# Attention inside two fused feed-forward layers: the two heads of a pair at partitions 0 and 64, scores as row tiles, outputs and kv as column tiles of the array

## The chip, the cores and the metric

One core of a Trainium2 chip runs one program. The metric is the device time of one execution in microseconds (us); shorter is better. The engines are called as in the profile: PE is TensorE's matmul side and PEld its weight loads, DVE is VectorE, ACT is ScalarE, POOL is GpSimd, and SP issues most DMAs.

## What is computed

The reference, cut to what matters (4 batches, 8 heads, 768 tokens, head size 48; all inputs are given in 32-bit floats except the four weight matrices, which are 64-bit floats):

```python
for t in range(S):
    state = alpha[:, :, t, :, None] * state + einsum('bhd,bhe->bhde', k[:, :, t], v[:, :, t])
    y[:, :, t] = einsum('bhd,bhde->bhe', q[:, :, t], state)
x = y.transpose(0, 2, 1, 3).reshape(3072, 384)
h = x @ w_in                 # 384 -> 2048
g = where(h >= 1, h, where(h <= -1, 0, (h + 1) ** 2 / 4))
x = g @ w_out                # 2048 -> 384
h = x @ w2_in; out = maximum(0.01 * h, h) @ w2_out
```

## The kernel before

**The two layers.** The 3,072 tokens are cut into 24 chunks of 128, three chunks to a tile of 384 columns, so eight tiles a layer. For each tile `gemm_in` (L451, matmuls on L460) makes 16 slices of the hidden layer, each with nine matmuls of 384 columns (three pieces of the contraction, three passes of a high and a low part of the operands), and `gemm_out` (L482, matmuls on L500 in the first layer and L502 in the second) adds each slice to the output with nine more. The non-linear function and the split into high and low part (L471 to L478) run on ACT, DVE and POOL. The 64-bit weights become 32-bit ones on ACT, DVE and POOL (`tick`, L207; the helpers at L27 to L40): the first layer's while the first tile is worked on, the second layer's later.

**The attention.** A chunk c belongs to batch c % 4. It is worked as seven or eight stages, for the eight heads as four pairs; R = 96 is the size of a pair, two heads of 48 side by side on the partitions. `st_alpha` (L274) transposes alpha on PE into a PSUM bank (tile `Tal`, L263), and DVE makes from it the running products in two sets of scans, `kt` (L278) and `qt` (L290), with the chunk's total `tot` and its bookkeeping in `good` (L286) between them; POOL scales the running state by `tot` (L293). The scans `qt` are the last to read the bank of `Tal`. `st_k` and `st_q` transpose k and q (`Tk`, `Tq`) and multiply. `st_qab` (L306) makes on ACT two copies of q, each with the other head of the pair set to zero (through the 0/1 mask `bdm`), so that a matmul over all 96 partitions gives the scores of one head. `st_scores` (L325) does this in two halves of two pairs: a matmul of 256 columns takes both heads, and DVE multiplies by the causal mask into `S` (L336). `st_ktok` transposes the keys back, `st_kv` (L342) multiplies keys and values of a pair (96 by 96, of which `bdm` keeps two blocks on DVE, L362) and POOL adds the result to the state (L363). `st_y` (L366) makes the outputs from the state (L374) and from `S` and `vpad` (L376), which holds each head's v with 48 columns of zeros beside it; ACT and DVE write them as high and low part into `xt`, the input of the first layer, and three small DMAs per chunk carry the fourth pair to the partitions from 96 up.

**What sets the order.** PE's order is the program's (a manual schedule for PE; the other engines' orders are made by a scheduler). The first three chunks stand in the list PRE ahead of the layers. From then on the stages of STEADY are dealt out over 27 half-steps to three chunks, one group of nine layer matmuls to a half-step: `slot = i * SLOTS // cnt`, in which cnt is the number of stage words. After the first stretch the attention's PSUM tiles come from a pool of three banks in turn, one bank to a tile (two halves of the scores are two tiles); a new tile waits until the last reader of the tile three before it is done:

```python
"al.0 q.0 qab.0 al.1 t k.0 sc0.0 k.1 sc1.0 t q.1 qab.1 t kt.0 "
...
STEADY = "al.1 sc0.0 k.1 sc1.0 qq.1 kt.0 y.0 kv.0"
```

## Time and profile before

| what | value |
|---|---|
| median of 3 runs (lowest, highest) | 1026.54 us (1025.8, 1028.24) |
| the profiled execution: its time, its span | 1027.63 us, 1026.0 us |
| PE, busy share of the span | 985.7 us, 96% |
| PEld | 965.3 us, 94% |
| DVE | 483.3 us, 47% |
| ACT | 492.0 us, 48% |
| POOL | 397.6 us, 39% |
| mean granted TensorE clock | 0.987 of full speed |
| chain of waits: PE, DVE, DMA | 86%, 6%, 3% of the span |

The span runs from the first to the last instruction of the profiled execution. A matmul of 32-bit floats outside the layers runs as two passes, each with its own weight load, so a group of two matmuls stands as x4 in the trace. Matmuls are pipelined, and a record covers more time than the array is taken up: what a group costs is read from the distance between starts, not from its own length. The first matmul after a group of another kind is recorded some 0.03 us after that group's last pass started, and its own successor shows the true pace.

### The profile page before, as it was taken

Reading aid. Unit: us, or ns where it says so; the run is one execution under the profiler, and the core shown is the slowest. Engines: PE = TensorE matmul, PEld = TensorE weight load, DVE = VectorE, ACT = ScalarE, POOL = GpSimd, SP = SyncE. Lnnn points to the kernel's source line nnn. Section 1 sums busy time; section 2 is a strip of 40 time slices with the busy share of each in tenths; the row PEclk is TensorE's granted clock in tenths of the full one; section 3 lists DMA queues with packets and bytes.
Section 4 is the critical chain, followed back from the end, with each engine's and each line's share of the span. In section 5 each row is a group of like instructions: output and inputs, shape, how many; then the busy total and the mean of one; then the engine's idle time right before and its main releaser. Section 6 shows DMA issues by size and latency. Waiting matters only on the chain.

```text
span 1026.0 us, 15727 instructions
## 1 busy us (share of the span) xinstructions
PE 985.7 (96%) x5874; PEld 965.3 (94%) x5874; DVE 483.3 (47%) x965; ACT 492.0 (48%) x966; POOL 397.6 (39%) x402
## 2 busy tenths in 40 slices
PE   6688799999999999999999999999999999999997
PEld 5587699999999999999999998999999999999997
DVE  7999955456475556555553445232322212121211
ACT  4476654554555465555555773333333333333332
POOL 2477843344434343433333333333333333333332
PEclk9799899999999999999999999999999999999999
DMA  9865542133344253342322435120201000000000
GB/s 190 197 147 138 135 111 47 35 100 88 91 110 104 72 137 87 99 105 76 98 61 62 130 101 167 32 70 24 70 30 40 15 10 23 1 24 1 24 1 27
DMA packets 133651, 78.95 MB, mean 77 GB/s; under 512 B 104384, under 2 KB 122304, under 8 KB 133568
## 3 DMA queue, kind: packets, MB, share of 16 engines
q1 hardware_dynamic: 121472, 52.71, 21.4%
q10 hardware_dynamic: 12096, 25.17, 7.9%
q8 instruction: 48, 0.79, 0.3%
q14 instruction: 35, 0.29, 0.1%
HBM read 59.77 MB, written 15.73 MB: 74 GB/s over the span
## 4 chain that ended last, share of the span: by engine, by line
PE 86%; DVE 6%; DMA 3%; issue 2%; POOL 1%; ACT 1%; SPq 1%; POOLq 0%; ACTq 0%; DVEq 0%
PE h L460 37%; PE acc L502 19%; PE acc L500 18%; PE sc L329 3%; PE y L376 3%; PE y L374 2%; DVE z L40 1%; DMA raw<-in_moe_w_in 1%; PE kv L350 1%; DMA ends<-in_alpha 1%; POOL z L35 1%; DVE z L31 1%; PE Tal L263 1%; PE Tq L263 1%; DVE good L528 1%
## 5 line engine op out<-in xcount | busy, mean ns | idle before, releaser
L460 PE MATMUL h<-xt,wi 128*128 128x384 f32 x2304 | 458.7, 343 | 8.3 <-DVE wi L183 3.2
L478 POOL TENSOR_TENSOR gg<-t,gg 128x384 fp32r<-128x384 f32 x256 | 268.6, 1050 | 490.8 <-ACT gg L477 484.7
L460 PEld LDWEIGHTS h<-xt,wi 128*128 128x128 f32 x2304 | 405.2, 189 | 12.8 <-DVE wi L183 3.8
L500 PE MATMUL acc<-gg,wo 128*128 128x384 f32 x1152 | 234.1, 347 | 0.2 <-POOL gg L478 0.2
L502 PE MATMUL acc<-wo,gg 128*128 128x384 f32 x1152 | 223.5, 338 | 0.0
L477 ACT ACTIVATE gg<-t 128x384 fp32r<-128x384 f32 x256 | 134.2, 525 | 183.3 <-DVE t L473 105.3
L502 PEld LDWEIGHTS acc<-wo,gg 128*128 128x128 f32 x1152 | 205.2, 188 | 0.0
L500 PEld LDWEIGHTS acc<-gg,wo 128*128 128x128 f32 x1152 | 202.5, 189 | 1.9 <-POOL gg L478 0.5
L476 DVE TENSOR_TENSOR t<-h,t 128x384 f32<-128x384 f32 x128 | 71.1, 557 | 272.9 <-ACT t L475 272.9
L475 ACT ACTIVATE t<-h 128x384 f32<-128x384 f32 x128 | 62.9, 492 | 180.4 <-PE h L460 180.4
L473 DVE SCALAR_TENSOR_TENSOR t<-t,h 128x384 f32<-128x384 f32 x128 | 70.2, 548 | 118.4 <-ACT t L472 113.5
L471 ACT ACTIVATE t<-h,half 128x384 f32<-128x384 f32 x128 | 73.8, 577 | 76.2 <-PE h L460 61.2
L35 POOL TENSOR_TENSOR z<-z,raw 128x384 int32<-128x384 int32 (+1 forms) x56 | 68.6, 1224 | 62.2 <-DVE z L32 39.0
L472 ACT ACTIVATE t<-t 128x384 f32<-128x384 f32 x128 | 67.1, 524 | 4.0 <-ACT t L471 1.0
L329 PE MATMUL sc<-qab,kt 96*128 96x256 f32 x192 | 54.7, 410 | 12.8 <-DVE S L336 5.7
L376 PE MATMUL y<-S,vpad 128*96 128x128 f32 x384 | 55.9, 272 | 2.1 <-DVE S L336 2.1
L329 PEld LDWEIGHTS sc<-qab,kt 96*128 96x128 f32 x192 | 38.2, 206 | 17.7 <-DVE S L336 6.3
L376 PEld LDWEIGHTS y<-S,vpad 128*96 128x96 f32 x384 | 46.4, 162 | 2.8 <-DVE S L336 2.8
L40 DVE SCALAR_TENSOR_TENSOR z<-raw,z 128x384 int32<-128x384 int32 (+1 forms) x56 | 44.6, 796 | 3.9 <-POOL z L35 1.6
L29 ACT ACTIVATE raw<-raw 128x384 int32<-128x384 uint32 (+1 forms) x56 | 33.7, 602 | 17.3 <-DMA raw<-in_moe_w_in 12.9
L31 DVE TENSOR_SCALAR z<-z 128x384 f32<-128x384 f32 (+1 forms) x56 | 30.5, 544 | 22.8 <-ACT z L30 22.6
L278 DVE TENSOR_TENSOR_SCAN kt<-Tal,zcol 96x127 f32<-96x127 f32 x96 | 32.4, 396 | 14.1 <-PE Tal L263 14.1
(69 smaller groups left out, 669.4 us busy)
## 6 DMA issues: line engine op xcount, KB each, us to landing
raw<-in_moe_w_out SPq DMA_DIRECT2D x16, 384.0 KB, 3.2
raw<-in_moe_w_in ACTq DMA_DIRECT2D x12, 512.0 KB, 4.2
raw<-in_moe_w_out ACTq DMA_DIRECT2D x16, 384.0 KB, 3.3
nat<-in_alpha SPq DMA_DIRECT2D x24, 192.0 KB, 3.2
nat<-in_k SPq DMA_DIRECT2D x24, 192.0 KB, 4.3
nat<-in_q SPq DMA_DIRECT2D x24, 192.0 KB, 4.5
vpad<-in_v SPq DMA_DIRECT2D x48, 96.0 KB, 2.6
raw<-in_moe_w_in SPq DMA_DIRECT2D x12, 384.0 KB, 4.5
```

The lines of the kernel that those rows point to most:

```text
L35: add_eng.tensor_tensor(out=z, in0=z, in1=low, op=ALU.add)
L329: nc.tensor.matmul(ps[:, i].rearrange("p e t -> p (e t)"), cs[c]["kt"][:, a, :], cs[c]["qab"][:, a].rearrange("p e t -> p (e t)"),)
L376: nc.tensor.matmul(y[:, a, :], vp[:, 2 * a + e, :], d["S"][:, a, e, :], start=first and e == 0, stop=e == 1)
L460: nc.tensor.matmul(h, w[:, wl, kk, f0:f0 + 128], xt[:, kk, xl, :], start=cnt == 0, stop=cnt == 3 * KD - 1,)
L471: nc.scalar.activation(out=t, in_=h, func=ACTF.Relu, bias=half, scale=0.5)
L472: nc.scalar.activation(out=t, in_=t, func=ACTF.Square)
L473: gi = nc.vector.scalar_tensor_tensor(out=g, in0=t, scalar=1.0, in1=h, op0=ALU.min, op1=ALU.max)
L476: gi = nc.vector.tensor_tensor(out=g, in0=h, in1=t, op=ALU.max)
L477: hi = nc.scalar.activation(out=gg[:, HI], in_=g, func=ACTF.Copy)
L478: lo = nc.gpsimd.tensor_tensor(out=gg[:, LO], in0=g, in1=gg[:, HI].bitcast(F32), op=ALU.subtract)
L500: nc.tensor.matmul(acc[d][:, :N], w[:, wl, mi, d * 128:(d + 1) * 128], gg[:, xl], start=st, stop=sto)
L502: nc.tensor.matmul(acc[d][:, :DM], gg[:, xl, d * C:(d + 1) * C], w[:, wl, mi, :], start=st, stop=sto)
```

## The change

The heads of a pair lie at partitions 0 and 64 (HP = 64; R is now 112, with 16 unused partitions between, X = 16). Scores: one matmul per head over 48 partitions, 128 columns, the two heads of a pair in different halves of the array's rows (a tile of 64 by 128) and into two banks, all eight in one stage; the copies `qab`, their mask and the stage `qab` are gone. Outputs from `S`: one matmul per head with 64 or 48 output rows in different halves of the array's columns (a tile of 128 by 64), after the four matmuls with the state. kv: likewise, per head 48 columns, and DVE adds into the two blocks of the state itself (ACT copies them for the first four chunks). POOL scales the state in two halves. alpha, k and q land in three fixed tiles with 64 places to a head, whose gaps POOL sets once; v is one DMA per chunk instead of two; the pieces of the first weight matrix come in four DMAs instead of two, and six small DMAs per chunk instead of three move the fourth pair. The pools of the attention are closed when it is done, and the pool `natp` is opened in their place.

```diff
-    R = 2 * D
+    HP = 64
+    R = HP + D
+    X = HP - D
...
+    states = [stp.tile([R, NP, R], F32, name=f"state{i}") for i in range(B)]
+    vs = [stp.tile([128, H, HP], F32, name=f"v{i}") for i in range(2)]
+    nats = [stp.tile([128, 3, H, HP], F32, name=f"nat{i}") for i in range(3)]
+    heads = [slice(HP * e, HP * e + D) for e in range(2)]
...
-            r3 = KD * R + 32 * i
-            (cq if layer else nc.sync).dma_start(out=t[:R], in_=wsrc[layer, kind][i * R:(i + 1) * R, cols])
-            (cq if layer else nc.sync).dma_start(out=t[R:], in_=wsrc[layer, kind][r3:r3 + 32, cols])
+            for e in range(2):
+                r0, r1 = (2 * i + e) * D, (2 * KD + e) * D + X * i
+                nc.sync.dma_start(out=t[HP * e:HP * e + D], in_=wsrc[layer, kind][r0:r0 + D, cols])
+                nc.sync.dma_start(out=t[HP * e + D:HP * e + HP], in_=wsrc[layer, kind][r1:r1 + X, cols])
...
-            nc.gpsimd.tensor_tensor(out=st, in0=st, in1=tot.to_broadcast([R, NP, R]), op=ALU.mult)
+            for h in heads:
+                nc.gpsimd.tensor_tensor(
+                    out=st[h, :, h], in0=st[h, :, h], in1=tot[h].to_broadcast([D, NP, D]), op=ALU.mult
+                )
...
-        for e in range(2):
-            nc.scalar.activation(out=qab[:, :, e, :], in_=qt, func=ACTF.Copy, scale=bdm[:, e * D:e * D + 1])
...
-    def st_scores(c, hf):
-        ps = bank("sc").rearrange("p (a e t) -> p a e t", a=2, e=2)
...
+    def st_scores(c):
+        kt, qt = cs[c]["kt"], cs[c]["qt"]
+        ps = [bank(f"sc{e}") for e in range(2)]
+        for a in range(NP):
+            for e, h in enumerate(heads):
+                nc.tensor.matmul(ps[e][:, a * C:(a + 1) * C], kt[h, a, :], qt[h, a, :])
+        S = sp.tile([128, 2, NP, C], F32, tag="S", name="S")
+        for e in range(2):
+            nc.vector.tensor_tensor(
+                out=S[:, e],
...
-            nc.tensor.matmul(
-                ps[:R, a * R:(a + 1) * R],
...
+            for e in range(2):
+                n = D if e else HP
+                nc.tensor.matmul(
+                    kv[HP * e:HP * e + n, a, :],
+                    cs[c]["kn"][:, a, HP * e:HP * e + n],
+                    vs[c % 2][:, 2 * a + e, :D],
+                )
         st = states[c % B]
-        if c < B:
-            nc.vector.tensor_tensor(out=st, in0=kv, in1=bd, op=ALU.mult)
-        else:
-            kvd = sp.tile([R, NP, R], F32, tag="kvd", name="kvd", bufs=1)
-            nc.vector.tensor_tensor(out=kvd, in0=kv, in1=bd, op=ALU.mult)
-            nc.gpsimd.tensor_tensor(out=st, in0=st, in1=kvd, op=ALU.add)
+        for h in heads:
+            if c < B:
+                nc.scalar.activation(out=st[h, :, h], in_=kv[h], func=ACTF.Copy)
+            else:
+                nc.vector.tensor_tensor(out=st[h, :, h], in0=kv[h], in1=st[h, :, h], op=ALU.add)
...
-        for a in (3, 0, 1, 2):
-            if not first:
-                nc.tensor.matmul(y[:, a, :], states[c % B][:, a, :], d["qt"][:, a, :], start=True, stop=False)
+        if not first:
+            for a in range(NP):
+                nc.tensor.matmul(
+                    y[:, a, :], states[c % B][:, a, :], d["qt"][:, a, :],
...
+        for a in range(NP):
             for e in range(2):
+                n = D if e else HP
                 nc.tensor.matmul(
-                    y[:, a, :], vp[:, 2 * a + e, :], d["S"][:, a, e, :], start=first and e == 0, stop=e == 1
+                    y[HP * e:HP * e + n, a, :], vs[c % 2][:, 2 * a + e, :n], d["S"][:, e, a, :],
...
-    STEADY = "al.1 sc0.0 k.1 sc1.0 qq.1 kt.0 y.0 kv.0"
+    STEADY = "al.1 sc.0 k.1 q.1 kt.0 y.0 kv.0"
```

With seven words instead of eight a chunk still takes nine half-steps, and the words move within them. On PE, between the transposes of k and of q of one chunk (`h` and `acc` are the groups of the layers; `Tal` of the same chunk stands two such groups and one scores stage ahead of `Tk` in both), before:

```order
L500 MATMUL acc_1571<-gg,wo_1162 128x384
L263 MATMUL Tk<-ident,nat 96x128 x4
L460 MATMUL h<-xt,wi_258 128x384 x9
L329 MATMUL sc<-qab,kt 128x256 x2
L500 MATMUL acc_1569<-gg,wo_1162 128x384 x3
L500 MATMUL acc_1570<-gg,wo_1162 128x384 x3
L500 MATMUL acc_1571<-gg,wo_1162 128x384 x3
L263 MATMUL Tq<-ident,nat 96x128 x4
L460 MATMUL h<-xt,wi_258 128x384 x9
L318 MATMUL ktok<-ident,kt 128x96 x4
```

and in the changed kernel:

```order
L494 MATMUL acc_1637<-gg,wo_1221 128x384
L267 MATMUL Tk<-ident,nat_128 112x128 x4
L454 MATMUL h<-xt,wi_267 128x384 x9
L267 MATMUL Tq<-ident,nat_128 112x128 x4
L494 MATMUL acc_1635<-gg,wo_1221 128x384 x3
L494 MATMUL acc_1636<-gg,wo_1221 128x384 x3
L494 MATMUL acc_1637<-gg,wo_1221 128x384 x3
L454 MATMUL h<-xt,wi_267 128x384 x9
L318 MATMUL ktok<-ident,kt 128x112 x4
```

The second half of the scores has left this place: `Tq` comes one layer group and a half of the scores earlier, and both halves of the scores stand together in the stage between `Tal` and `Tk`. Since each half takes a bank, `Tk` is now the third tile after `Tal` and gets its bank, where before the second half of the scores got it.

The outputs on PE, with the state (L374, now L369) and with `S` (L376), before:

```order
L374 MATMUL y<-qt,state_123 96x128
L376 MATMUL y<-S,vpad_127 96x128 x2
L374 MATMUL y<-qt,state_123 96x128
L376 MATMUL y<-S,vpad_127 96x128 x2
L374 MATMUL y<-qt,state_123 96x128
L376 MATMUL y<-S,vpad_127 96x128 x2
L374 MATMUL y<-qt,state_123 96x128
L376 MATMUL y<-S,vpad_127 96x128 x2
L460 MATMUL h<-xt,wi_258 128x384 x9
L350 MATMUL kv<-vpad_127,kn 96x96 x4
```

and in the changed kernel:

```order
L369 MATMUL y<-qt,state_122 112x128 x4
L376 MATMUL y<-S,v_126 64x128
L376 MATMUL y<-S,v_126 48x128
L376 MATMUL y<-S,v_126 64x128
L376 MATMUL y<-S,v_126 48x128
L376 MATMUL y<-S,v_126 64x128
L376 MATMUL y<-S,v_126 48x128
L376 MATMUL y<-S,v_126 64x128
L376 MATMUL y<-S,v_126 48x128
L454 MATMUL h<-xt,wi_267 128x384 x9
L349 MATMUL kv<-v_126,kn 64x48
L349 MATMUL kv<-v_126,kn 48x48
```

The number of matmuls of the outputs is the same (four with the state, eight with `S`), the first four of them now come first, and the eight go in turn to the two halves of the columns; kv has eight matmuls of 48 columns for four of 96.

On POOL, where the state is scaled (`gg` is the low part of a layer's hidden slice, `z` a piece of weights), with the semaphores that each row waits for, before:

```order
L363 TENSOR_TENSOR state_125<-state_125,kvd 96x384 [waits DVE_49]
L478 TENSOR_TENSOR gg<-t,gg 128x384 [waits Activation_49]
L293 TENSOR_TENSOR state_123<-state_123,tot 96x384 [waits DVE_49]
L478 TENSOR_TENSOR gg<-t,gg 128x384 [waits PE_49,Activation_49] x2
L276 MEMSET kt 96x4 [waits PE_49]
```

and in the changed kernel:

```order
L472 TENSOR_TENSOR gg<-t,gg 128x384 [waits PE_49,Activation_49]
L298 TENSOR_TENSOR state_123<-state_123,tot 48x4x48 [waits DVE_49]
L298 TENSOR_TENSOR state_123<-state_123,tot 48x4x48 [waits Pool_49]
L472 TENSOR_TENSOR gg<-t,gg 128x384 [waits PE_49,Activation_49,Pool_49]
L472 TENSOR_TENSOR gg<-t,gg 128x384 [waits PE_49,Activation_49]
```

The one scaling of 384 elements has become two of 192, the second waits for the first's own semaphore, and the addition of kv (L363) is gone from POOL.

## Rows read from the trace of the kernel before

**Rows 1.** Stretches: us, then busy us of PE, PEld, DVE, ACT, POOL; PEclk, DMA share, GB/s

```profile
0.00:137.00 137.00, 105.72 (x589) 93.88 (x590) 121.16 (x244) 81.94 (x165) 84.98 (x86) 0.91 0.72 163
137.00:512.00 375.00, 375.00 (x2404) 368.24 (x2403) 210.09 (x470) 203.15 (x396) 143.59 (x156) 1.00 0.35 88
```

**Rows 2.** Timeline of PE over one chunk: start us, length us, engine, line, operation

```profile
207.64 0.60 PE L263 MATMUL Tal<-ident,nat 128*96 128x128 f32 x4
...
209.67 1.03 PE L329 MATMUL sc<-qab,kt 96*128 96x256 f32 x4
...
212.12 0.60 PE L263 MATMUL Tk<-ident,nat 128*96 128x128 f32 x4
...
216.60 0.60 PE L263 MATMUL Tq<-ident,nat 128*96 128x128 f32 x4
...
218.62 0.49 PE L318 MATMUL ktok<-ident,kt 96*128 96x96 f32 x4
...
220.57 0.38 PE L374 MATMUL y<-qt,state 96*96 96x128 f32 x2
220.79 0.60 PE L376 MATMUL y<-S,vpad 128*96 128x128 f32 x4
...
224.79 0.84 PE L350 MATMUL kv<-vpad,kn 128*96 128x96 f32 x8
...
227.07 1.75 PE L460 MATMUL h<-xt,wi 128*128 128x384 f32 x9
228.66 0.27 PE L263 MATMUL Tal<-ident,nat 128*96 128x128 f32 x1
```

**Rows 3.** Timeline around L536, whose matmul has one output row (128*1)

```profile
964.68 0.34 PE L502 MATMUL acc<-wo,gg 128*128 128x384 f32 x1
964.94 0.09 PEld L536 LDWEIGHTS good<-good,ones_r 128*1 128x1 f32 x2 [0.25 <-issue]
964.95 0.20 PE L536 MATMUL good<-good,ones_r 128*1 128x20 f32 x2
965.36 0.52 PE L460 MATMUL h<-xt,wi 128*128 128x384 f32 x2
```

**Rows 4.** Weight loads from 137 us on, by line: ns min/median/max

```profile
L329 PEld LDWEIGHTS sc<-qab,kt x136: 186/188/193, 138.6 to 517.2; 96*128 96x128 f32 x136
L376 PEld LDWEIGHTS y<-S,vpad x256: 161/162/164, 149.8 to 505.3; 128*96 128x96 f32 x128
```

**Rows 5.** Timelines of PE and DVE after a `Tal`, an undisturbed chunk

```profile
249.67 0.60 PE L263 MATMUL Tal<-ident,nat 128*96 128x128 f32 x4
252.18 0.79 DVE L286 SCALAR_TENSOR_TENSOR good<-tot,good 96x4 f32<-96x4 f32 x1
252.90 1.59 DVE L290 TENSOR_TENSOR_SCAN qt<-Tal,rtot,zcol 96x128 f32<-96x128 f32 x4
```

**Rows 6.** Timelines of PE, DVE and POOL after a `Tal`, a disturbed chunk

```profile
157.72 0.60 PE L263 MATMUL Tal<-ident,nat 128*96 128x128 f32 x4
160.56 1.77 DVE L286 SCALAR_TENSOR_TENSOR good<-tot,good 96x4 f32<-96x4 f32 x1
162.25 1.59 DVE L290 TENSOR_TENSOR_SCAN qt<-Tal,rtot,zcol 96x128 f32<-96x128 f32 x4
160.51 0.83 POOL L293 TENSOR_TENSOR state<-state,tot 96x384 f32<-96x384 f32 x1 [2.95 <-DVE tot L284]
161.29 1.01 POOL L478 TENSOR_TENSOR gg<-t,gg 128x384 fp32r<-128x384 f32 x1
```

**Rows 7.** L286 from 137 us on: count, ns min/median/max

```profile
L286 DVE SCALAR_TENSOR_TENSOR good<-tot,good x17: 500/792/1967, 139.6 to 513.9; 96x4 f32<-96x4 f32 x17
```

**Rows 8.** Groups of instructions, by form, first 137 us: busy us, mean ns

```profile
L359 DVE TENSOR_TENSOR state<-kv,bdm 96x384 f32<-96x384 f32 x4 | 2.2, 542 | 0.0
L310 ACT ACTIVATE qab<-qt,bdm 96x512 f32<-96x512 f32 x14 | 9.3, 713 | 10.0 <-DVE qt L304 10.0
```

**Rows 9.** Chain of waits, opening: start us, us, what

```profile
8.86 0.42 SPq L159
```

More of the change, by code (lines that the diff above doesn't have):

```diff
@@ L101, in fast_path, with to_second @@
     pt = ctx.enter_context(tc.tile_pool(name="pt", bufs=3, space=bass.MemoryType.PSUM))
+    first = ctx.enter_context(ExitStack())
+    rawp = first.enter_context(tc.tile_pool(name="rawp", bufs=3))
+    tp = first.enter_context(tc.tile_pool(name="tp", bufs=2))
+    sp = first.enter_context(tc.tile_pool(name="sp", bufs=2))
+    stp = first.enter_context(tc.tile_pool(name="stp", bufs=1))
+    second = {}
+    def to_second():
+        first.close()
+        second["natp"] = ctx.enter_context(tc.tile_pool(name="natp", bufs=3, reuse_waits="tile"))
     x2d = dram.tile([128, KD, NT], F32, name="x2d")
@@ L113, in fast_path @@
     warm = const.tile([128, 1], F32, name="warm")
-    states = [const.tile([R, NP, R], F32, name=f"state{i}") for i in range(B)]
-    vpad = [const.tile([128, H, R], F32, name=f"vpad{i}") for i in range(2)]
-    nat = {}
+    states = [stp.tile([R, NP, R], F32, name=f"state{i}") for i in range(B)]
+    vs = [stp.tile([128, H, HP], F32, name=f"v{i}") for i in range(2)]
+    nats = [stp.tile([128, 3, H, HP], F32, name=f"nat{i}") for i in range(3)]
+    heads = [slice(HP * e, HP * e + D) for e in range(2)]
     fetched = set()
@@ L193, in load_z @@
         else:
-            t = natp.tile([128, DM], F32, tag="nat", name="zo")
+            t = second["natp"].tile([128, DM], F32, tag="nat", name="zo")
         cq.dma_start(out=t, in_=wz[kind, g][i])
@@ L304, in st_q @@
         nc.vector.tensor_tensor(out=qt, in0=ps, in1=qt, op=ALU.mult)
-    def st_qab(c):
-        qt = cs[c]["qt"]
-        qab = tp.tile([R, NP, 2, C], F32, tag="qab", name="qab", bufs=1)
-        for e in range(2):
-            nc.scalar.activation(out=qab[:, :, e, :], in_=qt, func=ACTF.Copy, scale=bdm[:, e * D:e * D + 1])
-        cs[c]["qab"] = qab
     def st_ktok(c):
@@ L388, in st_y @@
             for kk in range(KD):
-                nc.sync.dma_start(
-                    out=xt[R:, kk, :, cols].bitcast(F32), in_=xs[32 * kk:32 * kk + 32, :, :].bitcast(F32)
-                )
+                for e in range(2):
+                    nc.sync.dma_start(
+                        out=xt[HP * e + D:HP * e + HP, kk, :, cols].bitcast(F32),
+                        in_=xs[HP * e + X * kk:HP * e + X * (kk + 1), :, :].bitcast(F32),
+                    )
     tilesA = [(3 * i, 3) for i in range(NCH // 3)]
@@ L521, in alpha_ends @@
         w = B * H * S * D // (128 * NE)
-        t = natp.tile([128, w], F32, tag="nat", name="ends")
+        t = second["natp"].tile([128, w], F32, tag="nat", name="ends")
         nc.sync.dma_start(
@@ L544, in load_x2 @@
         xt = get_xt((1, j), n)
-        x = natp.tile([128, KD, N], F32, tag="nat", name="x2r")
+        x = second["natp"].tile([128, KD, N], F32, tag="nat", name="x2r")
         nc.sync.dma_start(out=x, in_=x2d[:, :, c0 * C:c0 * C + N])
@@ L589, in fast_path @@
         nc.scalar.activation(out=warm, in_=half, func=ACTF.Relu)
-        for t in vpad:
-            tv = t.rearrange("p (a two) (z d) -> p a two z d", two=2, z=2)
-            for e in range(2):
-                nc.vector.memset(tv[:, :, e, 1 - e, :], 0.0)
-        bt = bdm
-        ones.memset(bt, 1.0)
-        ones.affine_select(out=bt[:, :D], in_=bt[:, :D], pattern=[[0, D]], compare_op=ALU.is_ge, fill=0.0, base=D - 1, channel_multiplier=-1)
-        ones.affine_select(out=bt[:, D:], in_=bt[:, D:], pattern=[[0, D]], compare_op=ALU.is_ge, fill=0.0, base=-D, channel_multiplier=1)
+        for t in vs:
+            nc.vector.memset(t[:, :, D:], 0.0)
+        for t in states:
+            nc.vector.memset(t, 0.0)
+        for t in nats:
+            ones.memset(t[:, 0, :, D:], 1.0)
+            ones.memset(t[:, 1:, :, D:], 0.0)
         pos = 0
```

61 lines of the change are left out of this document (17 added, 44 removed), and 3 rows, old and new, of the table PRE.

## The prediction

> **What bounds the kernel now.** I read the table of stretches first, then PE's timeline over one chunk, then the timelines of DVE and POOL at the places where PE will wait for them. From 137 to 512 us PE is busy without a gap [rows 1]: 375.00 of 375.00 us, the clock at its full 2.4 GHz, no other engine over 60%. There a microsecond taken from PE's queue is a microsecond of the run, and one added, or waited, likewise. Before 137 us DVE is the busy engine (121.16 of 137 us, PE 105.72): weights are converted and PE waits, so less PE work buys nothing there. After 512 us there is no attention (its last matmuls start at 505 [rows 4]). The layers' own matmuls are unchanged.
>
> One chunk in the middle stretch shows what the attention takes from PE [rows 2]. A layer group of nine matmuls goes from 227.07 to 228.66, 1.59 us. `Tq` to `ktok` is 2.02 us with one such group, so four transposes take 0.43. `Tal` to `Tk` is 4.48 with two layer groups, so half of the scores takes 0.87, both 1.74. `ktok` to `y` is 1.95: 0.36. `y` to kv is 4.22: 2.63 for 24 passes, 0.11 each, of which the 16 with `S` take 1.75. kv to the next `Tal` is 3.87: 0.69.
>
> **What the change does on PE, per chunk.** The passes do not become fewer or shorter: 16 of 128 columns for the scores (before, 8 of 256), 16 of 128 for the outputs with `S`, 16 of 48 for kv (before, 8 of 96). A gain can come only from the array working on two halves at a time. No row shows that, so I bound it: without overlap a pass of 128 columns costs its 0.11; with full overlap two passes share it. A head has two passes, and PE keeps its order, so the second pass of one head can run beside the first of the next: 16 passes then take 9 steps, not 8. I take the overlapped end, because the pairs share neither rows (scores) nor columns (outputs, kv), and because loads and matmuls of different passes already run side by side: a load of 96 columns lasts 0.162 us by its record [rows 4] and the passes still follow every 0.11.
>
> Against it stands the price of going to a smaller tile and back, which one place shows [rows 3]. The matmul on L536 has one output row. Its weight load starts 0.26 us after the start of the last layer matmul, and from that start to the second layer matmul behind it are 0.68 us. Two ordinary distances are 2 x 0.177 (1.59 / 9), its own two tiny passes some 0.05: 0.28 us is lost, an unhidden load of 128 columns on the way out included. The first load on the way in comes on top: loads of 128 and 96 columns differ by 26 ns [rows 4], 0.8 ns a column, so some 0.10 for 128 columns and 0.05 for 64. Three groups per chunk pay this:
>
> - scores: 0.28 + 0.10 + 9 x 0.11 = 1.37 instead of 1.74: -0.37
> - outputs with `S`: 0.28 + 0.05 + 9 x 0.11 = 1.32 instead of 1.75: -0.43 (the passes with the state are as before)
> - kv: a pass of 48 columns streams for some 0.04, its load takes 0.05: 0.28 + 0.05 + 9 x 0.05 = 0.78 instead of 0.69: +0.09
> - `ktok` has 112 columns for 96: 0.36 x 112 / 96, +0.06. The other transposes stream the same 128 columns.
>
> That is -0.65 for a chunk with kv and -0.80 for the last four, which have neither kv nor `ktok`. From 137 us on there are 14 and 4: -9.1 and -3.2, together -12.3 us.
>
> **The new wait.** `Tk` now needs the bank of `Tal`, which DVE frees with its last `qt` scan. From the start of `Tal` to `Tk` PE will have 4.48 - 0.87 + 1.37 = 4.98 us. In an undisturbed chunk the scans end at 252.90 + 1.59 = 254.49, 4.82 after `Tal` [rows 5]: just in time. In a disturbed one they end at 163.84, 6.12 after it [rows 6], and PE would stand 1.14 us with all its queue behind it. The reason is `good`, an operation on four numbers per partition: it starts 0.05 after POOL's scaling of the state and ends only when that and the `gg` straight behind it are over, 1.77 us; where POOL has the scaling alone it takes 0.79 [rows 5]. So DVE gets through only when POOL pauses. The change cuts the scaling into two, the second waiting for the first's semaphore: that is a pause after about half of 0.83. Its price is not in the trace: between 0 (DVE gets through after 0.42, `good` at some 0.45, the scans some 1.3 us earlier, at 4.8) and the full 1.14 per disturbed chunk. I take the pause, since a wait of POOL for itself must let its first half finish. About eight of the 17 chunks that begin in this stretch are disturbed (the median of `good`, 0.792, is still the undisturbed value, the longest 1.967 [rows 7]), some by weight conversions that DVE takes in between; for those, and for `Tq`, which needs the first scores' bank after `Tk`, I leave 3.5 us.
>
> **Beside PE.** Before 137 us DVE loses four operations (`state<-kv`, 2.2 us [rows 8]), which go to ACT, and ACT loses 9.3 us of `qab` that stood between DVE and the scores. Against that SP issues more: six more DMAs ahead of the first conversions, at 0.42 each [rows 9], 2.5 us if none were hidden. I take -2.5 for the stretch, bounds +2.5 and -7 (DVE's 2.2 and half of `qab`'s 9.3). From 137 us on ACT (54%), POOL (38%) and DVE's two half additions for `kvd` are covered by PE; they matter only through the wait above. The DMAs of v and of the fourth pair fall in the same stretch and have most of a chunk's 21 us to land.
>
> **Sum.** -12.3 + 3.5 - 2.5 = -11.3. The profiled execution took 1027.63 us, 1.1 above the median of 1026.54; its span is 1026.0. 1027.63 - 11.3 - 1.1 gives **1015 us** as a median. A measurement of this kernel tells some 0.2%, 2 us, from no change.
>
> **Rivals.**
>
> *The halves do not run side by side.* The tiles are named, but each pass still takes its turn. Then scores are 0.38 + 16 x 0.11 = 2.14 (+0.40), outputs +0.34, kv 0.33 + 16 x 0.05 = 1.13 (+0.44), `ktok` +0.06: +1.24 in 14 chunks, +0.74 in four, 20.3 us; less 2.5: **1044**, slower. For it: no row shows two matmuls at once, and three entries and exits per chunk are certain. The point that decides is the length of a step of two passes: PE breaks even at (4.18 - 0.39 - 0.33 - 0.78 - 0.06) / 18 = 0.146 us, between 0.11 and 0.22.
>
> *Loads take turns, matmuls overlap.* Two loads of 128 columns need 0.21, so the scores gain nothing (+0.40); 64 and 48 columns need 0.09, less than the 0.11 of a step, so outputs keep -0.43; kv goes at 0.09 a pair, 0.33 + 8 x 0.09 = 1.05 (+0.36). With `ktok` +0.39 in 14 chunks and -0.03 in four, 5.3 us, no wait for `Tk`, less 2.5: **1029**. The Trainium skill (TensorE: Matmul & The Clock Gate, "LDWEIGHTS (loading the stationary operand)") has the time of a load go by its columns and not its rows, as rows 4 have it; the same skill (TensorEngine Tiling (Array Packing), "Key Properties") says that different tiles load and multiply in parallel, which speaks against this rival. No run here shows either for two tiles.
>
> *DVE does not get through in POOL's pause.* Then the disturbed chunks wait for `Tk`: eight times some 1.2 us, 9.6, with the 3.5 for the rest: -12.3 + 13.1 - 2.5 = -1.7, **1025**: PE's gain is eaten by the bank that DVE holds. For it: in rows 6 POOL starts `gg` without a pause and DVE is passed over. Against it: there POOL did not wait for itself. The Trainium skill (TensorEngine Tiling (Array Packing), "PSUM Bottleneck") warns that tiling speeds up TensorE and not the emptying of PSUM; that would be this case.
>
> **How the numbers follow.** The forecast gets 0.40, DVE passed over 0.17, loads in turn 0.19, no overlap 0.15, and 0.09 is left for an opening or a wait that goes otherwise (it may go either way). The forecast's own range is 1008 (no waits left, the opening at its better bound) to 1021. The range over the cases is 1008 to 1042: it holds the first three and leaves out most of the last. Faster by over 0.2%: 0.40 + a third of 0.17 + half of 0.09 and a little from loads in turn, 0.51, which I cut to 0.48 for what I cannot see; same 0.13; slower 0.39.
>
> **What would show it.** Starts of `sc` passes 0.05 us apart on average and a chunk's period of 20.4 us for 21.0 say that the halves overlap; 0.11 apart, with a period over 22 us, that they do not. Weight loads starting 0.26 us after the last layer matmul at each of the three groups confirm the price of a tile; at once, as elsewhere, refute it. `good` at 0.45 us confirms the pause, at 0.9 or 1.8 the third rival, with PE waiting for `qt` ahead of `Tk`. PE's last gap before the dense stretch earlier than 137 us confirms the opening. I am wrong if a step of two passes takes over 0.146 us, or if the dense stretch has waits of over 12 us.

## The result and the profile after

| | before | after |
|---|---|---|
| median | 1026.49 us (4 runs) | 1011.07 us (4 runs, 1010.6 to 1013.11) |
| ratio, 95% interval | | 0.9851 (0.9832 to 0.987) |
| profiled execution: time, span | 1027.63, 1026.0 us | 1010.68, 1008.9 us |

The time fell by 15.4 us, and the forecast of 1015 us lies 4 us beside it. That nearness is partly luck. The table cuts both spans where the same group of `h` begins (one group for each slice of the hidden layer; the 16th stands ahead of the dense stretch, at the 112th no attention is left).

| stretch of the span | before | after | difference | predicted |
|---|---|---|---|---|
| start to group 16 | 137.08 us | 142.79 us | +5.7 | -2.5 |
| group 16 to 112 | 419.66 | 405.40 | -14.3 | -8.8 |
| of it the attention's groups, waits for `Tk` included | 116.07 | 104.02 | -12.05 | -8.8 |
| of it the layers' own matmuls | 303.6 | 301.4 | -2.2 | 0 |
| group 112 to the end | 469.2 | 460.7 | -8.5 | 0 |

The attention gained more than forecast, the opening lost instead of gaining, and 8 to 9 us come from where nobody had looked: the pace of the layers' own matmuls.

From the page of the changed kernel, its span, busy times and the shares of the chain of waits:

```profile
span 1008.9 us, 16606 instructions
...
PE 956.6 (95%) x6226; PEld 923.7 (92%) x6226; DVE 469.3 (47%) x979; ACT 467.3 (46%) x926; POOL 385.8 (38%) x409
...
PE 81%; DVE 7%; DMA 4%; ACT 2%; SPq 2%; issue 2%; POOL 1%; ACTq 0%; DVEq 0%; POOLq 0%
```

PE is busy 29 us less and is off the chain of waits more often than before (81% for 86%). The stretches, with the columns of [rows 1]:

```profile
0.00:143.00 143.00, 100.22 (x687) 90.03 (x688) 116.80 (x244) 77.80 (x159) 84.95 (x90) 0.83 0.66 156
143.00:512.00 369.00, 366.37 (x2688) 346.32 (x2687) 208.17 (x499) 186.18 (x367) 135.34 (x163) 1.00 0.34 89
512.00:700.00 188.00, 187.01 (x1107) 184.99 (x1107) 72.83 (x119) 95.41 (x190) 63.26 (x61) 1.00 0.28 87
700.00:950.00 250.00, 250.00 (x1445) 249.70 (x1444) 61.44 (x100) 89.79 (x176) 85.12 (x81) 1.00 0.08 25
```

The dense stretch, 375.00 of 375.00 us in [rows 1], now has 2.63 us of gaps in 369. In the opening no engine is full: DVE is busy 116.80 of 143 us, where it had 121.16 of 137. The last row becomes important below: 1,445 matmuls in 250 us without any attention.

The timeline of PE over one chunk, to be laid beside [rows 2]:

```profile
300.22 0.60 PE L267 MATMUL Tal<-ident,nat 128*112 128x128 f32 x4
...
302.34 1.16 PE L330 MATMUL sc<-qt,kt 48*128 48x128 f32 x16
303.43 1.84 PE L454 MATMUL h<-xt,wi 128*128 128x384 f32 x9
305.17 0.65 PE L267 MATMUL Tk<-ident,nat 128*112 128x128 f32 x4
...
310.83 0.55 PE L318 MATMUL ktok<-ident,kt 112*128 112x112 f32 x4
...
312.80 1.04 PE L369 MATMUL y<-qt,state 112*112 112x128 f32 x8
313.77 1.09 PE L376 MATMUL y<-S,v 128*64 128x128 f32 x16
...
316.56 0.67 PE L349 MATMUL kv<-v,kn 128*64 128x48 f32 x16
...
320.40 0.60 PE L267 MATMUL Tal<-ident,nat 128*112 128x128 f32 x4
```

The 16 passes of the scores begin at 302.34, and the next layer group at 303.43. Taken singly from the trace, they start in pairs: 302.342 and 302.349, 302.555 and 302.562, then a pair every 0.105 to 0.112 us, eight steps for 16 passes, of which the first is twice as long. The outputs with `S` do the same (313.771 and 313.778, the next pair 0.15 us on, then a pair every 0.109 us). From `Tal` to `Tal` are 20.18 us with nine layer groups in between, 21.0 before. The Trainium skill (TensorEngine Tiling (Array Packing), "Key Properties") says that different tiles load and multiply in parallel; the trace agrees, 7 ns apart.

Each group's cost beyond the layers' matmuls around it (from the start of the last layer matmul ahead to the second behind, less two distances of 0.1733 us), median per chunk:

| group | before | after | difference | predicted |
|---|---|---|---|---|
| scores | 1.738 us | 1.297 us | -0.44 | -0.37 |
| outputs, passes with the state included | 2.645 | 2.096 | -0.55 | -0.43 |
| kv | 0.707 | 0.794 | +0.09 | +0.09 |
| `ktok` | 0.371 | 0.405 | +0.03 | +0.06 |
| `Tal`, `Tq` | 0.44 each | 0.44 each | 0 | 0 |
| `Tk`, sum of 17 | 7.55 | 11.57 | +4.0 | +3.5 |

The price of a tile shows at the weight load of the scores (timeline of PEld, same chunk):

```profile
302.34 0.97 PEld L330 LDWEIGHTS sc<-qt,kt 48*128 48x128 f32 x16 [0.25 <-issue]
```

It starts 0.266 us after the last layer matmul (302.074) and not at once, as predicted from [rows 3] with 0.26. The first pass of kv stands 0.27 us behind its layer matmul as well; that of the outputs with `S`, which follows a pass with the state, 0.20 us.

### The profile page after: what moved, and what is told of

It is laid out like the page before. It is cut to its first block, busy times and chain, and to the rows that moved or that the text cites. A ratio compares the mean times of both kernels' runs of the same rounds, so it can differ in the third digit from the quotient of the medians.

```text
span 1008.9 us, 16606 instructions
## 1 busy us (share of the span) xinstructions
PE 956.6 (95%) x6226; PEld 923.7 (92%) x6226; DVE 469.3 (47%) x979; ACT 467.3 (46%) x926; POOL 385.8 (38%) x409
## 4 chain that ended last, share of the span: by engine, by line
PE 81%; DVE 7%; DMA 4%; ACT 2%; SPq 2%; issue 2%; POOL 1%; ACTq 0%; DVEq 0%; POOLq 0%
PE h L454 36%; PE acc L496 19%; PE acc L494 17%; PE y L376 2%; PE sc L330 2%; PE y L369 2%; DVE z L40 1%; DMA raw<-in_moe_w_in 1%; DVE kt L282 1%; PE Tk L267 1%; DMA raw<-in_moe_w_out 1%; DMA x2r<-x2d 1%; DVE qt L294 1%; DVE z L31 1%; PE kv L349 1%
## 5 line engine op out<-in xcount | busy, mean ns | idle before, releaser
L494 PE MATMUL acc<-gg,wo 128*128 128x384 f32 x1152 | 231.1, 344 | 0.2 <-ACT o L507 0.2
L496 PE MATMUL acc<-wo,gg 128*128 128x384 f32 x1152 | 220.0, 334 | 0.0
L496 PEld LDWEIGHTS acc<-wo,gg 128*128 128x128 f32 x1152 | 201.5, 188 | 0.0
L40 DVE SCALAR_TENSOR_TENSOR z<-raw,z 128x384 int32<-128x384 int32 (+1 forms) x56 | 44.6, 797 | 8.5 <-POOL z L35 6.9
L31 DVE TENSOR_SCALAR z<-z 128x384 f32<-128x384 f32 (+1 forms) x56 | 27.2, 485 | 25.3 <-ACT z L30 25.2
L294 DVE TENSOR_TENSOR_SCAN qt<-Tal,rtot,zcol 112x128 f32<-112x128 f32 x96 | 38.3, 458 | 0.0
L282 DVE TENSOR_TENSOR_SCAN kt<-Tal,zcol 112x127 f32<-112x127 f32 x96 | 32.6, 400 | 12.2 <-PE Tal L267 11.2
L330 PEld LDWEIGHTS sc<-qt,kt 48*128 48x128 f32 x384 | 25.9, 204 | 12.5 <-issue 8.8
L330 PE MATMUL sc<-qt,kt 48*128 48x128 f32 x384 | 30.7, 303 | 6.0 <-DVE qt L311 3.2
L30 ACT ACTIVATE z<-raw 128x384 f32<-128x384 f32 (+1 forms) x56 | 33.2, 592 | 0.0
```

Source lines behind the costliest of these rows:

```text
L330: nc.tensor.matmul(ps[e][:, a * C:(a + 1) * C], kt[h, a, :], qt[h, a, :])
L494: nc.tensor.matmul(acc[d][:, :N], w[:, wl, mi, d * 128:(d + 1) * 128], gg[:, xl], start=st, stop=sto)
L496: nc.tensor.matmul(acc[d][:, :DM], gg[:, xl, d * C:(d + 1) * C], w[:, wl, mi, :], start=st, stop=sto)
```

## Experiments

### Why the layers' own matmuls got faster

Between 700 and 950 us both kernels run the same instructions. The trace has 1,423 matmuls there before the change and 1,445 after: 175.7 and 173.0 ns for each. Singly, the changed kernel has 173 or 174 ns throughout this stretch; the kernel before repeats 173, 174, 175, 182, 176 (around 560 us, say), and its mean is 175 to 176.5 ns in every 20 us from 40 us to the end. What differs is where the tiles lie. The constants stand ahead of weights and moving tiles alike, so taking `bdm`, the states and the padded v out of them moves both by as much. The distance between the two changed because the pools of the attention, which lay between the weights (`wp`) and the moving tiles (`xp`), were moved behind them:

```diff
     wp = ctx.enter_context(tc.tile_pool(name="wp", bufs=1))
-    rawp = ctx.enter_context(tc.tile_pool(name="rawp", bufs=3))
     zp = ctx.enter_context(tc.tile_pool(name="zp", bufs=4))
-    natp = ctx.enter_context(tc.tile_pool(name="natp", bufs=3))
-    tp = ctx.enter_context(tc.tile_pool(name="tp", bufs=2))
-    sp = ctx.enter_context(tc.tile_pool(name="sp", bufs=2))
     xp = ctx.enter_context(tc.tile_pool(name="xp", bufs=2))
```

The distances below are counted from the sizes of the tiles; the trace has no addresses.

**before_shift.**

```diff
+    pad = ctx.enter_context(tc.tile_pool(name="pad", bufs=1))
+    nc.gpsimd.memset(pad.tile([128, 96], F32, name="gap"), 0.0)
     xp = ctx.enter_context(tc.tile_pool(name="xp", bufs=2))
```

> The kernel before, with one edit: a gap of 384 bytes per partition ahead of the pool of xt, so that xt, xs, t, gg and the o tiles lie 384 bytes higher in SBUF; instructions and waits are as before but for one tiny fill at the start. In the kernel before, the weight tiles begin at 800 modulo 1024 and the moving tiles (xt, gg) at 416; in the changed kernel both begin at 416; here both begin at 800. Theory of the placement: the layers' matmuls follow at 173.3 ns instead of 175.9 because weights and moving tile begin at the same offset. Then this kernel has 173.3 too, from its first matmul to its last; 4,300 layer matmuls behind 137 us by 2.6 ns are 11 us: 1015.3, though the attention is untouched. Rival, the pace comes from the changed passes themselves, or from where the tiles lie as a whole (in the kernel before the moving tiles begin above 182,000 bytes, in the changed one below 160,000): 175.9 ns and 1026.5 as before.

Measured: 1019.01 us, ratio to the kernel before 0.9921 (0.9906 to 0.9935): 8 of the 11 us expected. Among the attention's groups the pace gains less than behind them: from 150 to 500 us the mean goes from 176.1 to 175.1 ns, from 560 us on from 175.9 to 173.3. **after_shift** is the same edit on the changed kernel with `[128, 160]`.

> The changed kernel with a gap of 640 bytes per partition ahead of the pool of xt: weights begin at 416 modulo 1024 and the moving tiles at 32, which is the distance of 384 that they have in the kernel before. Theory of the placement: the layers' matmuls fall to 175.9 ns a piece also where there is no attention, and the time goes from 1011.1 to about 1021 (some 11 us, less what the waits for Tk's bank take up). Rival, the pace belongs to the new passes or to the low addresses: 173.3 ns and 1011.1.

Measured: 1024.14 us, ratio 0.997 (0.9958 to 0.9981). The stretch without attention, of the kernel before, of before_shift and of after_shift, in this order (columns as above):

```profile
700.00:950.00 250.00, 250.00 (x1423) 250.00 (x1422) 60.75 (x97) 89.31 (x173) 84.05 (x80) 1.00 0.08 24
```

```profile
700.00:950.00 250.00, 250.00 (x1445) 250.00 (x1444) 61.26 (x98) 90.39 (x176) 85.11 (x80) 1.00 0.07 24
```

```profile
700.00:950.00 250.00, 250.00 (x1423) 250.00 (x1422) 60.72 (x97) 88.98 (x173) 83.26 (x80) 1.00 0.08 24
```

The pace goes with the gap both ways, at full clock, with the attention of either kernel and with the moving tiles high or low in SBUF. From group 16 to group 254, before_shift is 8.8 us shorter than the kernel before, and after_shift 8.4 us longer than the changed one; the rest of the 13 us there is a later opening (147.66 us at group 16), whose cause is open.

**eight_distances** asks which distances matter.

```diff
+            if layer == 0 and (kind, g) != ("i", 0):
+                nc.gpsimd.memset(wp.tile([128, 32], F32, tag=f"gap{kind}{g}", name=f"gap{kind}{g}"), 0.0)
             W[layer, kind, g] = wp.tile(
```

> The changed kernel with a gap of 128 bytes per partition (filled once at the start) between each two weight tiles, so that the eight of them lie at eight distances from the moving tiles: modulo 1024 the first w_in tile 128, the first w_out 256, then 384, 512, 640, 768, 896 and, for the last w_out, 0. The layers' matmuls with each tile are read apart, where no attention is left (behind 560 us). Theory A, equal offsets are what counts: 173.3 ns with the last w_out tile only, 175 to 176 with the seven others; the time about 1022. Theory B, only some distances are bad (384 is the one seen): 173.3 with most and 176 with one to three of them; 1012 to 1016. Theory C, it is the layout as a whole and no distance of two tiles: one pace, the same with all eight.

Measured: one run, 1020.68 us, of which 4.6 are again a later opening (group 16 at 147.41 us), so the theories are told apart by the pace. From its timeline of PE, `h` (with w_in) and `acc` (with w_out) in turn:

```profile
700.97 1.75 PE L456 MATMUL h<-xt,wi 128*128 128x384 f32 x9
702.56 1.72 PE L498 MATMUL acc<-wo,gg 128*128 128x384 f32 x9
704.12 1.75 PE L456 MATMUL h<-xt,wi 128*128 128x384 f32 x9
```

Nine matmuls with w_in take 1.59 us, nine with w_out 1.56. Over everything behind 560 us, the four w_in tiles (distances 128, 384, 640, 896 modulo 1024) have 176.11, 176.11, 176.12 and 176.11 ns, the four w_out tiles (256, 512, 768, 0) 173.52, 173.59, 173.52 and 173.57. So theory B holds, with four bad distances: **173.5 ns where weights and moving tile begin a multiple of 256 bytes apart, 176.1 at an odd multiple of 128.** All the odd multiples fall on w_in here. That it is not the kind of weight follows from the other kernels: behind 560 us the changed one has 173.4 ns with w_in and 173.3 with w_out, the one before 175.6 and 176.3. Other distances than multiples of 128 were not tried, and why the chip does this stays open.

### Do the two halves really work at once?

**halves_in_turn.** In scores, outputs and kv:

```diff
-        for a in range(NP):
-            for e, h in enumerate(heads):
+        for e, h in enumerate(heads):
+            for a in range(NP):
```

> The changed kernel with the loops over heads and pairs swapped in scores, outputs and kv: all four matmuls of the upper half, then all four of the lower half. The same passes, the same tiles of the array, as many entries to a smaller tile; only neighbours in PE's queue now lie on the same half. Theory, the gain comes from two halves side by side: 16 passes take 16 steps instead of 8, so scores +0.8 us (7 to 8 steps of 0.105), outputs +0.8, kv +0.35 per chunk; over the 18 chunks of the dense stretch (14 with kv) 29 + 5 = 34 us, less up to 4 for the waits for Tk's bank, which vanish: 1041 to 1045, slower than the kernel before. Rival, the gain comes from shorter passes or loads of a smaller tile, whatever their order: within 2 us of 1011.1. In between (PE lets the last passes of one half run beside the first ones of the other only): 1 step in 16 is saved, 1040.

Measured: 1029.04 us, ratio 1.0019 (1.0009 to 1.0028). Its timeline of PE:

```profile
167.18 1.71 PE L330 MATMUL sc<-qt,kt 48*128 48x128 f32 x16
```

The same 16 passes take 1.71 us instead of 1.16. Per chunk the scores cost 0.54 us more, the outputs 0.48, kv 0.17, and the waits for `Tk` are gone: 18 us lost. The gain does come from the halves side by side, but the loss is only half to two thirds of what I expected. The single starts show why: the first five passes of the first half run alone, and right behind the start of the fifth (167.724) the second half starts too (167.730), with three passes of the first half still to come. 16 passes take 13 steps. Which half a pass belongs to is read from the semaphores: the load that waits for the second half's bank starts at 167.728, and the pass that signals the end of the first half's only at 168.059. So up to three passes of one half do not hold up the other; whether a half's own passes keep their order, the trace does not tell.

**kv_whole.** The one term that I had as a loss:

```diff
-        for a in range(NP):
-            for e in range(2):
-                n = D if e else HP
-                nc.tensor.matmul(
...
+        for a in range(NP):
+            nc.tensor.matmul(kv[:, a], cs[c]["kn"][:, a, :], vs[c % 2][:, 2 * a:2 * a + 2, :D])
```

> The changed kernel with kv as one matmul of the whole array for each pair (lhsT 112 columns, 96 columns of v), the blocks off the diagonal left unread, instead of two column tiles. Per chunk the group of kv costs 0.794 us beyond two ordinary distances in the changed kernel and 0.707 in the kernel before. Theory, a tiled group pays some 0.28 us for going to the smaller tile and back, which passes of 48 columns don't earn back: 0.70 to 0.77 here, weight load right behind the layer's matmul and not 0.27 later, 1 us over 14 chunks, no difference that can be measured in the time (1009.5 to 1011.5). Rival, the switch costs nothing of its own and the longer passes count: 0.85 or more, 1012.

Measured: 1012.27 us, ratio 0.9851 (0.9836 to 0.9866), the same as the changed kernel. Timeline of PE, then of PEld:

```profile
318.12 0.93 PE L347 MATMUL kv<-v,kn 128*112 128x96 f32 x8
```

```profile
317.94 0.94 PEld L347 LDWEIGHTS kv<-v,kn 128*112 128x112 f32 x8
```

The load stands right behind the layer's matmul, so the price of the tile is gone, but eight passes with loads of 112 columns cost 0.806 us, more than the 0.707 with 96 columns in the kernel before and as much as the tiled 0.794. Both theories are half right, and for kv the choice makes no difference.

### The wait for `Tk`

**one_scaling** undoes the cut of the scaling of the state:

```diff
-            for h in heads:
-                nc.gpsimd.tensor_tensor(
-                    out=st[h, :, h], in0=st[h, :, h], in1=tot[h].to_broadcast([D, NP, D]), op=ALU.mult
-                )
+            nc.gpsimd.tensor_tensor(out=st, in0=st, in1=tot.to_broadcast([R, NP, R]), op=ALU.mult)
```

> The changed kernel with the scaling of the state as one POOL operation over the whole tile of 112 partitions, as the kernel before has it, instead of one for each head. Theory, the pause of POOL between the two halves is what lets DVE's good through after 0.47 us: good then takes 0.8 to 1.0 us in an undisturbed chunk and 1.8 to 2.0 where gg or a conversion stands behind the scaling; the qt scans end 0.4 to 1.4 us later, and PE waits ahead of Tk in nearly every chunk of the dense stretch, 0.3 to 1.4 us each: 1011.1 + 7 to 14 = 1018 to 1025. Rival, good gets through for another reason or the scans have room: good at 0.47 or Tk without a wait, 1010 to 1012.

Measured: 1021.65 us, ratio 0.9948 (0.993 to 0.9966). `good` in the dense stretch (count, ns min/median/max), changed kernel first, then one_scaling; [rows 7] has 500/792/1967 before:

```profile
L290 DVE SCALAR_TENSOR_TENSOR good<-tot,good x17: 377/471/794, 145.4 to 506.2; 112x4 f32<-112x4 f32 x17
```

```profile
L290 DVE SCALAR_TENSOR_TENSOR good<-tot,good x16: 794/901/2064, 146.7 to 497.7; 112x4 f32<-112x4 f32 x16
```

In the changed kernel no `good` takes 1.77 us any more: POOL's first half ends 0.45 us after `good` has started, the second begins 0.08 us later, and in that pause DVE gets through. Without the pause, PE waits. Waits of PE from 143 to 512 us in the two kernels (us in total, times, longest):

```profile
PE Tk L267 <- DVE qt L294: 2.6, 4, 1.2
```

```profile
PE Tk L267 <- DVE qt L294: 9.5, 7, 2.0
```

10.6 us in the time for one POOL instruction instead of two (0.93 us for 0.50 each, with the unused blocks), on an engine that is busy 38%; 9.0 of it from group 16 to 112, 1.7 in the opening. This is the third rival of the prediction, made real. The Trainium skill (TensorEngine Tiling (Array Packing), "PSUM Bottleneck") warns that tiling does not speed up the emptying of PSUM; here it is the bank of `Tal`, held by DVE.

The waits that the changed kernel keeps have another cause. In the four chunks with the dearest `Tk` (0.94 to 1.90 us for 0.44), DVE takes weight conversions (L40, L31, L32) ahead of the `qt` scans; without one between `Tal` and the scans `Tk` costs 0.44 to 0.62. The dearest, timeline of DVE:

```profile
233.13 0.69 DVE L40 SCALAR_TENSOR_TENSOR z<-raw,z 128x512 int32<-128x512 int32 x1
...
235.01 0.47 DVE L290 SCALAR_TENSOR_TENSOR good<-tot,good 112x4 f32<-112x4 f32 x1
235.41 1.60 DVE L294 TENSOR_TENSOR_SCAN qt<-Tal,rtot,zcol 112x128 f32<-112x128 f32 x4
```

**scores_first** takes the remaining waits away by order:

```diff
-    STEADY = "al.1 sc.0 k.1 q.1 kt.0 y.0 kv.0"
+    STEADY = "sc.0 al.1 k.1 q.1 kt.0 y.0 kv.0"
```

> The changed kernel with the order of the stages of the steady part changed in one place: the scores of a chunk ahead of the transposes of the next alpha, not behind them. In the ring of three banks Tk then takes the bank of the first scores, and not that of Tal, which DVE holds until its last qt scan. Theory, the waits ahead of Tk (4.1 us over the 17 chunks from 143 to 512 us, five of them over 0.3 us) are waits for that bank: they go, Tk costs 0.44 in every chunk, and with the one at 103 us (5.1) up to 8 us go: 1003 to 1008. Rival, the wait only moves on, to ktok, which takes Tal's bank now, or to scores that stand right behind the q of their own chunk: 1010 to 1013, with the waits at sc or ktok.

Measured: 1009.38 us, ratio 0.9829 (0.9816 to 0.9843). `Tk` costs 0.435 us in each chunk, 7.41 in all for 11.57, and from group 16 to 112 the span is 4.0 us shorter. One new wait came in there, 0.7 us of `acc` for DVE's `o` (L505) at 492 us. The opening did not move (142.77 us at group 16 for 142.79), although its wait for `Tk` at 103 us (4.8 on PE, 5.1 on PEld) is gone: other waits stand in its place, so it was not this wait that bounded it. With 1.6 us given back behind group 112, the two intervals overlap; in the time the gain is not settled, in the stretch it is.

### The opening

PE's timeline shows the largest wait of PE in the opening, in the changed kernel:

```profile
41.37 0.65 PE L267 MATMUL Tal<-ident,nat 128*112 128x128 f32 x4 [2.85 <-ACT state L357]
50.00 3.22 PE L454 MATMUL h<-xt,wi 128*128 128x384 f32 x9 [7.98 <-DMA xt<-xs]
```

The moves of the fourth pair are late. The first group of `h` starts 1.8 us later than before (48.19), of the 5.7 us; the rest gathers behind it. What stands on SP there, changed kernel first, then the kernel before (start, us, line, operation):

```profile
44.75 0.42 SPq L163 DMA_DIRECT2D raw<-in_moe_w_in  x1
45.27 3.88 SPq L391 DMA_DIRECT2D xt<-xs  x6
49.20 0.58 SPq L162 DMA_DIRECT2D raw<-in_moe_w_in  x1
```

```profile
45.59 1.87 SPq L389 DMA_DIRECT2D xt<-xs  x3
47.58 0.51 SPq L158 DMA_DIRECT2D raw<-in_moe_w_in  x1
```

Six moves instead of three, at some 0.62 us each (0.60 in the kernel before, where [rows 9] has 0.42 for a load), and the weights' loads wait behind them. In the first 143 us SP issues 138 DMAs in 79.9 us, before 104 in 62.6. DVE's conversions then wait for their input (idle time ahead of two of their lines, changed kernel):

```profile
L40 DVE SCALAR_TENSOR_TENSOR z<-raw,z 128x384 int32<-128x384 int32 (+1 forms) x28 | 27.5, 986 | 8.5 <-POOL z L35 6.9 <-POOL kt L280 0.9 <-DMA nat<-in_q 0.7
L31 DVE TENSOR_SCALAR z<-z 128x384 f32<-128x384 f32 (+1 forms) x28 | 16.1, 574 | 5.8 <-ACT z L30 5.7
```

Before, the same two have 3.9 and 3.2 us of idle time. By these two lines DVE's shorter list bought nothing because the conversions' input came late.

The granted clock fell as well: 0.83 for 0.91 in the opening, by the rows of stretches here and in [rows 1]. Of its two levels, that is, worked out from these shares, some 49 us at 1.2 GHz for some 25. PE is on it behind its longest wait: the group of `h` behind the 7.98 us takes 3.22 us, a full-speed one behind the scores 1.84 (303.43 above). No run here parts what this adds to the later opening from the waits that bring it about.

**before_split** puts the added DMAs of weights and moves into the kernel before:

```diff
-            (cq if layer else nc.sync).dma_start(out=t[:R], in_=wsrc[layer, kind][i * R:(i + 1) * R, cols])
-            (cq if layer else nc.sync).dma_start(out=t[R:], in_=wsrc[layer, kind][r3:r3 + 32, cols])
+            for e in range(2):
+                p0, p1 = e * D, R + 16 * e
+                nc.sync.dma_start(out=t[p0:p0 + D], in_=wsrc[layer, kind][i * R + p0:i * R + p0 + D, cols])
+                nc.sync.dma_start(out=t[p1:p1 + 16], in_=wsrc[layer, kind][r3 + 16 * e:r3 + 16 * e + 16, cols])
```

(and each move `xt<-xs` in two of 16 partitions).

> The kernel before with as many DMAs as the changed kernel: each piece of the first layer's w_in in four DMAs instead of two (48, 48, 16 and 16 rows), each move of the fourth pair in two of 16 partitions instead of one of 32. Nothing else is touched. Theory of SP's queue: the changed kernel's later start of the dense stretch (the group of h that stands at 137.08 us in the kernel before stands at 142.79 there) comes from the issues on SP, 138 instead of 104 in the first 143 us, 79.9 us of issuing instead of 62.6, with the weights behind the moves. Then this kernel's group stands 4 to 7 us later, and the time is 1030 to 1034. Rival, the loss comes from the attention's stages (Tk waits for Tal's bank: 3.6 us at 77 and 5.1 at 103): within 1 us of the kernel before.

Measured: 1030.29 us, ratio 1.0031 (1.0021 to 1.0042); group 16 at 139.79 us, 2.7 later. "As many DMAs as the changed kernel" is not so: v keeps its two a chunk, and SP issues 146 in 85.9 us in the first 143 us, 8 more than the changed kernel. The 42 added DMAs cost 3.3 us, so the changed kernel's queue should explain no more than some half of its 5.7.

Four kernels take issues off SP. **moves_on_act** and **moves_on_pool** change the queue of half of the moves:

```diff
-                    nc.sync.dma_start(
+                    (nc.scalar if e and c < 7 else nc.sync).dma_start(
```

> The changed kernel with half of the moves (xt<-xs of the lower head, three DMAs a chunk) issued from ACT's queue for the first seven chunks, so that SP issues 21 DMAs fewer, 13 us of issuing, in the opening. Theory of SP's queue: the weights' DMAs behind the moves start 1.9 us earlier at each of the places on the chain of waits (45.3 to 49.2, 74 to 75.4), and the dense stretch begins 3 to 6 us earlier: 1006 to 1008. Rival, ACT at 54% of the opening becomes the late one (three issues of 0.6 us in front of its conversions), or DVE's conversions bound the stretch anyway: 1010 to 1013.

Measured: 1011.82 us, ratio 0.9853 (0.9838 to 0.9868): no change. Group 0 of `h` comes at 52.28 us for 50.00, and group 16 at 141.71 for 142.79.

> scores_first (1009.4 us) with half of the moves of the first seven chunks issued from POOL's queue. Theory of SP's queue: SP issues 13 us less, the weights start 1.9 us earlier behind each group of moves, 1005 to 1007. Rival, POOL, which adds the words of each conversion (DVE's longest wait in the opening is for it, 6.9 us), pays for the issues and hands its sums on later: 1010 to 1014.

Measured (the edit on scores_first, `nc.gpsimd`): 1013.18 us, ratio 0.9859 (0.9844 to 0.9874), 3.8 us slower than scores_first; group 0 at 55.87 us for 49.89. The time is the rival's; through which link POOL's issues cost it is not shown.

**wout_on_act** (on scores_first):

```diff
-            (cq if layer else nc.sync).dma_start(out=t, in_=src)
+            cq.dma_start(out=t, in_=src)
```

> scores_first (1009.4 us) with the first layer's w_out loads, one DMA each, issued from ACT's queue instead of SP's: SP is relieved of 16 issues, 7.3 us, ACT gets them. Theory of SP's queue: w_out pieces no longer stand behind moves and loads of the attention (the one issued at 87.0 us, 80.5 in the kernel before), and the dense stretch begins 2 to 5 us earlier: 1005 to 1007. Rival, ACT issues a load only when the conversions ahead of it in its own order are through, so the loads come later than from SP, as the moves did: 1009 to 1013.

Measured: **1004.77 us, ratio 0.9771 (0.9758 to 0.9784)**, the fastest kernel of this study and below the changed one's interval. Group 16 stands at 140.98 us, 1.8 earlier, and from group 112 to 254 the span is 1.8 us shorter as well (waits of 0.7 us for 1.8). The edit moves nothing in that stretch, so this part is not shown to be its work.

**win_half_on_act** goes on in the same way, with two of the four DMAs of each w_in piece:

```diff
+                eng = cq if e else nc.sync
-                nc.sync.dma_start(out=t[HP * e:HP * e + D], in_=wsrc[layer, kind][r0:r0 + D, cols])
+                eng.dma_start(out=t[HP * e:HP * e + D], in_=wsrc[layer, kind][r0:r0 + D, cols])
```

> wout_on_act (1004.8 us) with half of the first layer's w_in loads (the two DMAs of the lower head, 24 in all, some 11 us of issuing) also issued from ACT's queue, so that SP issues about as long in the opening as in the kernel before. Theory, SP's queue still holds up the weights: the dense stretch begins 1 to 4 us earlier than the 140.98 us of wout_on_act, 1001 to 1004. Rival, the opening is now bound by the chain of conversions through ACT, DVE and POOL, and ACT pays for 24 issues more: 1005 to 1009.

Measured: 1006.82 us, ratio 0.9805 (0.9791 to 0.9818), 2 us slower, although SP now issues 98 DMAs in 62.0 us, as long as in the kernel before. Group 16 stands at 142.87. So SP's queue explains 2 to 3 us of the opening's loss, by before_split and wout_on_act. The other half is not settled: the opening is a chain through SP, ACT, DVE and POOL, and moving one link shifts the rest. Each of these starts is from one traced execution, and kv_whole, whose edit changes nothing but kv there, has group 16 at 144.58 us, 1.8 later than the changed kernel; a difference of 2 us at group 16 alone is not safe.

## Why the prediction was right, and where it was not

**Side by side: right, and undersized.** I took the overlapped end, with 9 steps for 16 passes. It is 8: the two heads of one pair start together, not the second pass of one beside the first of the next. That is 0.11 us a group: -0.43 becomes -0.54 for the outputs (-0.55 measured) and -0.37 becomes -0.48 for the scores (-0.44 measured). The price of a tile was nearly right: 0.266 us to the first load, and the scores' 1.297 less eight steps of 0.11 is 0.42, of 0.38 predicted. The two rivals in which halves or loads take turns are refuted by the pairs of starts, and halves_in_turn shows what the overlap is worth. (In the rival with loads in turn, 0.38 + 8 x 0.21 makes +0.32 for the scores, not +0.40: 1028 instead of 1029.)

**kv and `ktok`: right**, +0.09 and +0.03 (+0.06 predicted).

**The wait for `Tk`: right**, +4.0 for 3.5. The assumption behind it, `good` at some 0.45 us in POOL's pause, is what the trace shows (0.471), and one_scaling has the price of its failing: 10.6 us, predicted as 9.6 more. What remains, 4.0, is mostly DVE's weight conversions. The prediction had named them and left 3.5 for them and `Tq` together without a sum, so that it fits so well is luck.

**The opening: wrong in sign.** The step that failed is "I take -2.5 for the stretch": it credited DVE's and ACT's lost work and took the six DMAs ahead of the first conversions as the whole of SP's side. SP's issues went up by 34 in the stretch, the moves at some 0.62 us each, and each group of moves stands ahead of weights. Some 2 to 3 of the +5.7 us are that queue; the cause of the rest stays open, the lower clock included. Its bound of +2.5 was too low as well, since it priced only the first pieces.

**"The layers' own matmuls are unchanged": wrong in the time.** The instructions are unchanged, their addresses are not. The distance of 0.177 (1.59 / 9) that I had read in [rows 2] as the layers' pace was itself a slowed one. By the two shifts it costs 8.4 to 8.8 us between group 16 and group 254, and it was no term of the sum.

So the sum came out near by cancelling, which is luck: the attention 3 us better than predicted, the opening 8 worse, the layers' own pace 9 better, with 2 us of smaller waits behind group 112. At the same bad distance the change is worth 0.3% (after_shift, ratio 0.997, its later opening of 4.9 us included), at the same good one 0.7 to 0.8% (1011.1 against 1019.0 us for before_shift); the change as it was written gives 1.5%, and about half of that belongs to the distance of two tiles.

## What to carry to other kernels

When a change moves pools, compare the time from start to start of matmuls that it does not touch, in a stretch that it does not touch, before putting the time down to the change; and where a matmul's weights and its moving tile begin an odd multiple of 128 bytes apart, try a gap. Tiles of the array pay when neighbours in the queue lie on different halves; write the loop so, and count the bank that an earlier stage still holds. Count issues on a shared queue at the places where something urgent stands behind them, not as a sum.

## What was not expected of the hardware

- The pace of a full-array matmul of 384 columns depends on the distance of its two operands in SBUF: 173.5 ns at multiples of 256 bytes, 176.1 at odd multiples of 128, at full clock (eight distances in one kernel, and a shift in each of the two others).
- PE lets passes of one half start ahead of up to three earlier passes of the other half (167.730 against 167.836 and later), though all stand in one queue.
- An operation of DVE that takes 0.13 us while POOL scales no state (`good` at 6.8 us) takes 0.47 us where POOL pauses for 0.08 us between two halves of the scaling, 0.90 where it scales in one piece and then stops, and up to 2.06 where its next operation follows without a pause.
